# Fewer changes of the array's form, the rows s = 0 with weights fixed, and a reordered head and tail in a Fourier-mixing and maxout kernel

## The chip, the cores and the metric

The kernel runs on one core of a Trainium2 chip. Its engines are TensorE (PE in the profile, with its weight loads as PEld), VectorE (DVE), ScalarE (ACT), GpSimd (POOL) and SyncE (SP, which here only issues DMAs). The metric is the device time of one execution in microseconds (us); of several runs the median is taken. The profile is that of one execution.

## The reference

```python
def _attn_ref(x):                      # x: (8, 3072, 256)
    X = np.fft.fft(x, axis=1)
    X = np.fft.fft(X, axis=2)
    return X.real.astype(np.float32)

def _moe_ref(x, w1, w2, w3, w_out):    # x: (24576, 256), w: (256, 768), w_out: (768, 256)
    h = np.maximum(np.maximum(x @ w1, x @ w2), x @ w3)
    return (h @ w_out).astype(np.float32)
```

The real part of a two-dimensional Fourier transform over 3072 rows and 256 columns is taken for each of 8 batches, and its 8 x 3072 rows go through a small network: three products with 768 columns each, the largest of the three at each place, and a product with `w_out`.

## The kernel before

The kernel folds the transform over the 256 columns into the weights: `w1`, `w2`, `w3` are multiplied once, in the head, by cosine tables (`g_all`, `gd_all`, `gw`). What is left for each batch is the transform over the rows, in stages, and the network.

**Stage one** (`Mix.s`, line 390) multiplies x by a table `tab` of 64 columns. Since 64 columns fill half of the 128 x 128 array, each of the pieces s0 to s5 is a pair of matmuls that run side by side in the two halves of the array (`tile_position=(0, 0)` and `(0, 64)`), 512 columns each. The piece s6 holds one single row of x that is left over and is one matmul of 128 columns in one half. A copy takes each piece out of PSUM. The stores `y0`, `y1` and the loads `z0`, `z1` (issued on SP) then turn the result by way of DRAM, and **stage two** (`Mix.k`) multiplies it by sine and cosine tables into `tE` and `tO`. The first row of each batch, s = 0, is kept apart in `t_mid` and is written alone (`out[S*b]`).

**The units.** A batch has 18 units: three blocks (`blk`) of 512 columns times six blocks of 128 hidden columns (`jc`). The loop at line 898 writes out the order of a unit by hand: `begin` (the products for the rows counted upwards, `hp`), `finish` of the unit before (those counted downwards, `hm`), `third` for a unit two further on, one scatter of finished rows at units 0, 4, 8 and 14 (`PACE`), ten steps of the product with `w_out` (`l2_some`), and then what the plan has for this unit (`at`, `piece`). All engines keep this order: each takes its instructions in the order of the program.

A unit is either *plain*, with six matmuls of 512 columns on TensorE (`unit_plus` four, `unit_minus` two), two relus on ACT and two maxima on DVE, or *split*, with five matmuls: `third` gives two of them to its own PSUM tiles `e3` and `d3`, DVE adds a rank-one term (`even3`), ACT scales (`odd3`), and POOL makes the sum and the difference of the two (`plus3`, `minus3`, line 867), which DVE then needs at lines 879 and 892. Odd units are split from unit 7 of batch 0 on; even ones where `EXTRA` says so: 12 and 14 in batch 0, then 0, 4, 8, 12 and 14, and 0, 4, 8 and 12 in the last batch.

The tiles `e3`, `d3`, those of stage one, of stage two and of the even part `pl` share three PSUM buffers (`ps_f`). The plain units and the split even units share one buffer for the third product (`ps_w3`), all odd ones and the plain ones two others (`ps_l1`).

**The plan of stage one.** For batch 0 the pieces of batch 1 lie in four units (`ahead0`). For the batches 1 to 6 the pieces of the next batch lie in three units (`ahead`): s0 and s1 in unit 1; s2, s3 and s6 in unit 2; s4 and s5 in unit 3.

**The rows s = 0** (`l2_mid`, line 620) are computed for all batches together in the last batch: hidden values in unit 1, the product with `gw` and `w_out` in unit 3. There the 8 values of a batch row are the weights (128 x 8) and `gw` or `wout_bf` stream, 256 columns in each of eight matmuls; one store of 8 rows follows.

**The head** (lines 150 to 330 and 674 to 739). POOL makes index ramps (`iota`, `ramp`) and issues all the loads; x of batch 0 comes in four parts, each of which DVE mirrors (`mirror`, line 124) before stage one of it can run. POOL also clears a part of the buffer `tb`, between two groups of weight loads. DVE makes the signs `sgn` and `dif` between two mirrors. Then DVE transposes `tb` (line 427), and the first units follow. POOL computes the last third of the angles (`angle`) after all that. `column` (line 348) turns one row of `g_all` into a column by six matmuls with a single row of the array.

**The tail.** In the last batch POOL makes two reversed copies of `tE` and `tO` at the start of unit 12 (line 911); `l2_last` uses them to write the last block in four parts, so that stores run while the rest is computed. The rows counted downwards leave by indirect DMAs from POOL (`scatter`, line 654); the last batch has one each at units 0, 4, 8, 14 and 16, and the rest at the end.

Of the kernel before, what the change touches and what calls it, by code (L numbers as in the profile page):

```python
# [30 lines left out]
PACE = (0, 4, 8, 14)  # L31
EXTRA = (12, 14), (0, 4, 8, 12, 14), (0, 4, 8, 12)

# [12 lines left out]
def kernel(  # L46
# [43 lines left out]
    x0u = consts.tile([128, 160], BF16, tag="x0u")  # L90
    tab = consts.tile([128, 64], BF16, tag="tab")
    tabx = consts.tile([128, 2 * RI], BF16, tag="tabx")
# [95 lines left out]
    for k in range(3):  # L188
        load_w(k, 0, 128)
    nc.gpsimd.memset(tbw[:, :, 24:32], 0)  # L190
    for k in range(3):
        load_w(k, 128, 384)
    ramp(2)

    zero = gen.tile([128, 512], BF16, tag="zero")
    nc.vector.memset(zero, 0.0)
    nc.vector.memset(x0u, 0.0)
    one = consts.tile([1, 1], BF16, tag="one")
    nc.vector.memset(one, 1.0)
    half_pi = gen.tile([128, 1], FP32, tag="half_pi")  # L200
    nc.vector.memset(half_pi, 0.5 * math.pi)
    nc.scalar.activation(out=half_pi, in_=half_pi, func=AX.Sin)
    nc.vector.memset(half_pi, 0.5 * math.pi)
    ang_o = gen.tile([128, NA], FP32, tag="ang_o")
    nc.vector.memset(ang_o, 0.0)
# [142 lines left out]
    def column():  # L348

        psc = ps_f.tile([128, 512], FP32, name="psc", tag="ps")  # L350
        for jc in range(NJC):
            nc.tensor.matmul(psc[:, jc:jc + 1], g_all[0:1, jc, 3, :], one, start=True, stop=True)
        nc.scalar.copy(out=wcol, in_=psc[:, 0:NJC])
# [27 lines left out]
    class Mix:  # L381
# [8 lines left out]
        def s(self, k, pool=ps_f, evict=nc.scalar.copy):  # L390
            ps1 = pool.tile([128, 512], FP32, name="ps1", tag="ps")
            if k < 6:
                for hh in range(2):
                    nc.tensor.matmul(ps1[hh * 64:hh * 64 + 64], tab,  # L394
                                     self.x[:, 8 * k + hh:8 * k + 8:2, 0:128],
                                     start=True, stop=True, tile_position=(0, 64 * hh))
                if self.b:
                    evict(out=tbv[:, 4 * k:4 * k + 4, :],
                          in_=ps1.rearrange("p (s f) -> p s f", s=4))
                else:  # L400
                    evict(out=tbt[:, :, 4 * k:4 * k + 4, :],
                          in_=ps1.rearrange("p (s f l) -> p f s l", s=4, l=2))
            else:
                nc.tensor.matmul(ps1[0:64, 0:128], tab, self.x[:, 48, 0:128],
                                 start=True, stop=True, tile_position=(0, 0))
                if self.b:
                    evict(out=tbv[0:64, 24, :], in_=ps1[0:64, 0:128])
                else:
                    evict(out=tbt[0:64, :, 24, :],
                          in_=ps1[0:64, 0:128].rearrange("p (f l) -> p f l", l=2))  # L410
# [209 lines left out]
    def l2_mid():  # L620
# [16 lines left out]
        po = ps_f.tile([128, 512], FP32, name="pom", tag="ps")  # L637
        for k in range(2):
            nc.tensor.matmul(po[0:B, 0:256], t_mid[:, k, :], gw[:, k * 256:(k + 1) * 256],
                             start=(k == 0), stop=(k == 1))  # L640
        for _ in l2_hidden(po[0:B, 0:256], lambda jc: hmid[:, jc, :]):
            pass
        ot = even_pool.tile([128, 512], FP32, name="even", tag="even")
        nc.vector.tensor_copy(out=ot[0:B, 0:256], in_=po[0:B, 0:256])
        store(nc.sync, out[0: S * (B - 1) + 1: S, :], ot[0:B, 0:256])

# [37 lines left out]
    warm_up(1)  # L684
    scal(sgn, pidx, 0.0, ALU.is_equal)
    scal(sgn, sgn, 2.0, ALU.mult, -1.0, ALU.add)
    scal(dif, sgn, 1.0, ALU.subtract)
    mirror(0, *FIRST[3])
# [48 lines left out]
    differ(0, 2, 128, 384)  # L737
    m.f()
    angle()

    def rows():

        pool = nc.gpsimd
        rows_f = gen.tile([128, 4], FP32, tag="rows_f")
        adj = gen.tile([128, 4], FP32, tag="adj")
        far = gen.tile([128, 1], FP32, tag="far")
        for (c, n, base, cm) in ((0, 2, 766, -8), (2, 1, 3069, -32), (3, 1, 3056, -16)):
            iota(rows_f[:, c:c + n], [[-1, n]], base=base, cm=cm)
        for (c, base, cm) in ((0, 766, 0), (1, 511, 0), (2, 1013, 0), (3, 1025, -16)):
            iota(adj[:, c:c + 1], [[0, 1]], base=base, cm=cm)  # L750
        scal(far, pidx, 96.0, ALU.is_ge, eng=pool)
        scal(adj, adj, far, ALU.mult, eng=pool)
        pool.tensor_tensor(out=rows_f, in0=rows_f, in1=adj, op=ALU.add)
        nc.gpsimd.tensor_copy(rows_m, rows_f)

# [65 lines left out]
    for b in range(2, B):  # L821
# [3 lines left out]
        for ch in range(8):  # L825
# [5 lines left out]
              15: ("v1", "kE1"), 16: ("kO2",), 17: ("v2", "kE2", "end")}  # L831
    ahead = {1: ("s0", "s1"), 2: ("s2", "y0", "s3", "s6"), 3: ("s4", "s5", "y1", "u"),
             5: ("z0", "z1"), 11: ("x",), 12: ("kO0",), 13: ("v0", "kE0", "kO1"),
# [64 lines left out]
    for g in range(B * UNITS):  # L898
# [20 lines left out]
        for lead in (1, 2):  # L919
            if is_split(g + lead) and (lead == 1) == (g + lead == 7):  # L920
                third(g + lead)
        if u in PACE or (b == B - 1 and u == 16):
            scatter(1)
        l2_some(10)
# [44 lines left out]
```

## Time and profile before

| | us |
|---|---|
| median of 3 runs (lowest, highest) | 386.15 (385.78, 387.81) |
| the profiled execution | 386.05 |
| its span, from the first to the last instruction | 384.2 |
| TensorE busy | 372.2 |
| DVE busy | 336.9 |
| POOL busy | 334.3 |
| ACT busy | 242.5 |

All times in the profile count from the start of the span. A line of a timeline gives start, length, engine, line of the code, operation, output and input, and in brackets the idle time of the engine just before, with the instruction that ended it. Matmuls overlap: the length of one is its flight, and the distance of two starts is what one costs in a stream. A line of the windows gives a stretch, its length, the busy time of PE, PEld, DVE, ACT and POOL with the count of instructions, the granted TensorE clock, the busy share of the DMA engines and the GB/s that they moved. A line of the waits gives engine and line, what it waited for, the total, the number and the longest; "issue" stands for idle time that nothing in the profile explains.

### The profile page before, as it was taken

The numbers are of one execution on the slowest core, as the hardware profiler recorded it, in microseconds if no ns is written. First come the engines' busy times: TensorE is split into PE (matmuls) and PEld (weight loads), VectorE is DVE, ScalarE is ACT, GpSimd is POOL, SyncE is SP. The second block draws the span as 40 slices with busy tenths as digits, with TensorE's granted clock in tenths as the row PEclk, the third lists the DMA queues.
The fourth block names the chain that finished last, engine by engine and source line by source line (L and its number), as shares of the span: only waits on it lengthen the run. The fifth ranks groups of instructions, "written<-read, shape, count | busy, mean of one in ns | idle before, by whom it ended". The sixth has DMA issues, their size and how long they took to land.

```text
span 384.2 us, 8003 instructions
## 1 busy us (share of the span) xinstructions
PE 372.2 (97%) x2785; PEld 234.6 (61%) x2785; DVE 336.9 (88%) x568; ACT 242.5 (63%) x454; POOL 334.3 (87%) x356
## 2 busy tenths in 40 slices
PE   6699999999999999999999999999999999999995
PEld 2354566566765667556665666666665667666674
DVE  7889798799897998989987998989987998989982
ACT  6877788567857686567766777567856535434430
POOL 9976599969999899989999899989988899888971
PEclk9999999999999999999999999999999999999999
DMA  8999836695279735595269825695213633212226
GB/s 117 169 185 164 160 117 97 202 156 178 73 155 199 203 113 115 161 218 176 69 123 199 214 105 124 179 182 183 93 56 124 178 129 97 73 67 97 97 80 209
DMA packets 51299, 54.13 MB, mean 141 GB/s; under 512 B 25813, under 2 KB 44268, under 8 KB 50563
## 3 DMA queue, kind: packets, MB, share of 16 engines
q0 software_dynamic: 19392, 26.45, 34.2%
q1 hardware_dynamic: 31334, 26.57, 25.7%
q10 hardware_dynamic: 532, 0.59, 0.5%
q8 instruction: 22, 0.36, 0.4%
q14 instruction: 19, 0.16, 0.1%
HBM read 36.95 MB, written 30.81 MB: 176 GB/s over the span
## 4 chain that ended last, share of the span: by engine, by line
PE 90%; DVE 3%; DMA 2%; ACT 2%; issue 1%; POOL 1%; DVEq 0%; POOLq 0%
PE po L550 32%; PE pse L494 10%; PE pse L487 8%; PE pse L877 6%; PE pse L878 6%; PE e L858 6%; PE d L860 6%; PE po L573 5%; PE ps L460 3%; PE ps L394 3%; PE pl L566 3%; DMA xt<-in_x_dram 2%; DVE yb L427 1%; ACT stmp L500 1%; PE psg L311 1%
## 5 line engine op out<-in xcount | busy, mean ns | idle before, releaser
L867 POOL TENSOR_TENSOR plus<-even,odd 128x512 bf16<-128x512 f32 x105 | 133.4, 1271 | 31.4 <-DVE even L863 25.8
L867 POOL TENSOR_TENSOR minus<-even,odd 128x512 bf16<-128x512 f32 x105 | 133.5, 1272 | 0.0
L862 ACT ACTIVATE odd<-d 128x512 f32<-128x512 f32 x105 | 62.7, 597 | 60.4 <-PE d L860 47.6
L879 DVE SCALAR_TENSOR_TENSOR hp<-pse,plus 128x512 bf16<-128x512 f32 x105 | 72.2, 687 | 25.0 <-PE pse L878 22.8
L550 PE MATMUL po<-wout_bf,hp 128*128 128x256 bf16 x576 | 86.1, 273 | 0.0
L550 PE MATMUL po<-wout_bf,hm 128*128 128x256 bf16 x576 | 78.6, 273 | 0.0
L863 DVE SCALAR_TENSOR_TENSOR even<-vb,wcol,e 128x512 f32<-128x512 bf16 x105 | 77.4, 737 | 0.0
L550 PEld LDWEIGHTS <-hp 128*128 128x128 bf16 x576 | 56.3, 98 | 26.2
L892 DVE SCALAR_TENSOR_TENSOR hm<-pse,minus 128x512 bf16<-128x512 f32 x105 | 71.4, 680 | 0.4
L550 PEld LDWEIGHTS <-hm 128*128 128x128 bf16 x576 | 56.3, 98 | 16.4
L494 PE MATMUL pse<-tO,gd_all 128*128 128x512 bf16 x183 | 63.1, 380 | 0.0
L500 ACT ACTIVATE stmp<-pse 128x512 bf16<-128x512 f32 x78 | 46.3, 599 | 21.2 <-PE pse L487 10.3
L578 DVE TENSOR_TENSOR kq<-po,even 128x512 f32<-128x512 f32 x60 | 41.0, 683 | 0.0
L129 ACT COPY xt<-xt 64x762 bf16<-64x762 bf16 (+1 forms) x48 | 39.8, 838 | 1.0
L877 PE MATMUL pse<-tE,g_all 128*128 128x512 bf16 x105 | 39.9, 380 | 0.1
L858 PE MATMUL e<-tE,g_all 128*128 128x512 bf16 x105 | 39.8, 379 | 0.0
L860 PE MATMUL d<-tO,gd_all 128*128 128x512 bf16 x105 | 39.8, 379 | 0.0
L878 PE MATMUL pse<-tO,g_all 128*128 128x512 bf16 x105 | 39.8, 379 | 0.0
L573 PE MATMUL po<-gw,tO 128*128 128x512 bf16 x92 | 34.9, 379 | 0.0
L570 ACT COPY even<-pl 128x512 f32<-128x512 f32 x46 | 26.8, 582 | 9.5 <-DVE kq L578 7.8
L501 DVE TENSOR_TENSOR hp<-pse,stmp 128x512 bf16<-128x512 f32 x39 | 26.8, 686 | 5.7 <-PE e L858 2.1
L494 PEld LDWEIGHTS <-gd_all 128*128 128x128 bf16 x183 | 17.9, 98 | 20.3 <-issue 2.5
(182 smaller groups left out, 500.2 us busy)
## 6 DMA issues: line engine op xcount, KB each, us to landing
db<-tb SPq DMA_DIRECT2D x21, 192.0 KB
xt<-in_x_dram POOLq DMA_DIRECT2D x5, 784.0 KB, 7.7
xt<-in_x_dram POOLq DMA_DIRECT2D x5, 752.0 KB, 8.6
out_dram<-obuf SPq DMA_DIRECT2D x8, 384.0 KB
out_dram<-kq SPq DMA_DIRECT2D x8, 384.0 KB
vb<-vd SPq DMA_DIRECT2D x23, 128.0 KB
out_dram<-kq SPq DMA_DIRECT2D x7, 288.0 KB
out_dram<-kq SPq DMA_DIRECT2D x15, 128.0 KB
```

The source lines that it names most:

```text
L494: nc.tensor.matmul(pse, gd_all[:, jc, i, :], to, start=False, stop=True, skip_group_check=True)
L550: nc.tensor.matmul(po, hcols(jc), wout_bf[:, jc * 256:(jc + 1) * 256], start=False, stop=(jc == NJC - 1), skip_group_check=True)
L573: nc.tensor.matmul(po, to[:, cp], gw[:, 256:768], start=True, stop=True)
L858: nc.tensor.matmul(e3, g_all[:, jc, 2, :], te, start=True, stop=True)
L860: nc.tensor.matmul(d3, gd_all[:, jc, 1, :], to, start=True, stop=True)
L862: nc.scalar.activation(out=odd3, in_=d3, func=AX.Copy, scale=-0.5)
L863: nc.vector.scalar_tensor_tensor(out=even3, in0=vb, scalar=wcol[:, jc:jc + 1], in1=e3, op0=ALU.mult, op1=ALU.add)
L867: nc.gpsimd.tensor_tensor(out=dst, in0=even3, in1=odd3, op=op)
L877: nc.tensor.matmul(pse2, g_all[:, jc, 0, :], te, start=True, stop=False)
L878: nc.tensor.matmul(pse2, g_all[:, jc, 1, :], to, start=False, stop=True)
L879: nc.vector.scalar_tensor_tensor(out=dst, in0=pse2, scalar=0.0, in1=sums[g][0], op0=ALU.max, op1=ALU.max)
L892: nc.vector.scalar_tensor_tensor(out=dst, in0=pses[0], scalar=0.0, in1=sums.pop(g)[1], op0=ALU.max, op1=ALU.max)
```

## The change

- `EXTRA`: unit 14 of the last batch is split as well.
- `tab` has 128 columns; `rows` (POOL, unit 5 of batch 0) copies the first 64 into the second 64. From batch 1 on the single row s6 is a matmul of the whole array, with 128 weight columns.
- `ahead`: s0, s1, s2 and y0 in unit 1; s3, s4, s5 in unit 2; s6, y1 and u in unit 3.
- `one` is a column of 128 with a one on top, and `column` uses the whole array.
- `l2_mid`: the blocks of `gw` and `wout_bf` (128 x 128) are the weights and the 8 values stream; sixteen matmuls give the result with the output columns on the partitions. DVE copies 128 x 16 values, and two stores write them with single elements of 4 bytes.
- Head: POOL's clearing of `tb` becomes a copy of zeros on ACT; `ramp(2)` moves from behind the weight loads to just before `angle`; the three instructions for `sgn` and `dif` move from DVE to POOL.
- `scatter`: the last batch has one each at units 0, 4 and 8 and two at unit 16; none at 14.

```diff
-EXTRA = (12, 14), (0, 4, 8, 12, 14), (0, 4, 8, 12)
+EXTRA = (12, 14), (0, 4, 8, 12, 14), (0, 4, 8, 12, 14)
...
-    tab = consts.tile([128, 64], BF16, tag="tab")
+    tab = consts.tile([128, 128], BF16, tag="tab")
...
-    nc.gpsimd.memset(tbw[:, :, 24:32], 0)
     for k in range(3):
         load_w(k, 128, 384)
-    ramp(2)
...
-    one = consts.tile([1, 1], BF16, tag="one")
-    nc.vector.memset(one, 1.0)
+    one = consts.tile([128, 1], BF16, tag="one")
+    nc.vector.memset(one, 0.0)
+    nc.vector.memset(one[0:1], 1.0)
...
+    nc.scalar.copy(out=tbt[:, :, 24:32, :], in_=zero[:, 0:16].rearrange("p (s l) -> p s l", l=2)
+                   .unsqueeze(1).to_broadcast([128, 64, 8, 2]))
...
-            nc.tensor.matmul(psc[:, jc:jc + 1], g_all[0:1, jc, 3, :], one, start=True, stop=True)
+            nc.tensor.matmul(psc[:, jc:jc + 1], g_all[:, jc, 3, :], one, start=True, stop=True)
...
-                    nc.tensor.matmul(ps1[hh * 64:hh * 64 + 64], tab,
+                    nc.tensor.matmul(ps1[hh * 64:hh * 64 + 64], tab[:, 0:64],
...
-                nc.tensor.matmul(ps1[0:64, 0:128], tab, self.x[:, 48, 0:128],
-                                 start=True, stop=True, tile_position=(0, 0))
+                n = 128 if self.b else 64
+                nc.tensor.matmul(ps1[0:n, 0:128], tab[:, 0:n], self.x[:, 48, 0:128],
+                                 start=True, stop=True)
...
-        for k in range(2):
-            nc.tensor.matmul(po[0:B, 0:256], t_mid[:, k, :], gw[:, k * 256:(k + 1) * 256],
-                             start=(k == 0), stop=(k == 1))
-        for _ in l2_hidden(po[0:B, 0:256], lambda jc: hmid[:, jc, :]):
-            pass
+        for h in range(2):
+            steps = [(gw[:, 256 * k + 128 * h:256 * k + 128 * h + 128], t_mid[:, k, :])
+                     for k in range(2)]
+            steps += [(wout_bf[:, 256 * jc + 128 * h:256 * jc + 128 * h + 128], hmid[:, jc, :])
+                      for jc in range(NJC)]
+            for k, (w, v) in enumerate(steps):
+                nc.tensor.matmul(po[:, h * B:h * B + B], w, v,
+                                 start=(k == 0), stop=(k == len(steps) - 1))
...
-        nc.vector.tensor_copy(out=ot[0:B, 0:256], in_=po[0:B, 0:256])
-        store(nc.sync, out[0: S * (B - 1) + 1: S, :], ot[0:B, 0:256])
+        nc.vector.tensor_copy(out=ot[:, 0:2 * B], in_=po[:, 0:2 * B])
+        for h in range(2):
+            store(nc.sync, out[0:S * (B - 1) + 1:S, 128 * h:128 * h + 128].rearrange("b p -> p b"),
+                  ot[:, h * B:h * B + B])
...
-    scal(sgn, pidx, 0.0, ALU.is_equal)
-    scal(sgn, sgn, 2.0, ALU.mult, -1.0, ALU.add)
-    scal(dif, sgn, 1.0, ALU.subtract)
+    scal(sgn, pidx, 0.0, ALU.is_equal, eng=nc.gpsimd)
+    scal(sgn, sgn, 2.0, ALU.mult, -1.0, ALU.add, eng=nc.gpsimd)
+    scal(dif, sgn, 1.0, ALU.subtract, eng=nc.gpsimd)
...
     m.f()
+    ramp(2)
     angle()
...
-        nc.gpsimd.tensor_copy(rows_m, rows_f)
+        pool.tensor_copy(rows_m, rows_f)
+        pool.tensor_copy(tab[:, 64:128], tab[:, 0:64])
...
-    ahead = {1: ("s0", "s1"), 2: ("s2", "y0", "s3", "s6"), 3: ("s4", "s5", "y1", "u"),
+    ahead = {1: ("s0", "s1", "s2", "y0"), 2: ("s3", "s4", "s5"), 3: ("s6", "y1", "u"),
...
-        if u in PACE or (b == B - 1 and u == 16):
-            scatter(1)
+        if b < B - 1:
+            scatter(u in PACE)
+        else:
+            scatter({0: 1, 4: 1, 8: 1, 16: 2}.get(u, 0))
```

## The prediction

> **What bounds the kernel now.** I read the page first (busy times, then the chain that ended last), then the table of windows for one batch in the middle.
>
> ```profile
> PE 372.2 (97%) x2785; PEld 234.6 (61%) x2785; DVE 336.9 (88%) x568; ACT 242.5 (63%) x454; POOL 334.3 (87%) x356
> ...
> PE 90%; DVE 3%; DMA 2%; ACT 2%; issue 1%; POOL 1%; DVEq 0%; POOLq 0%
> ```
> ```profile
> 92.52:136.37 43.85, 43.85 (x330) 27.78 (x329) 39.38 (x63) 30.93 (x57) 40.58 (x39) 1.00 0.66 158
> ```
> TensorE is busy for all 43.85 us of batch 2, at full clock (1.00), while DVE works 39.38 and POOL 40.58 us of them. So in the middle a shorter TensorE programme is a shorter kernel, as long as POOL and DVE, each with some 3 us to spare per batch, do not come to stand in front. Head and tail have other limits and are read on their own.
>
> What a matmul costs in a stream, from the chain in order of time:
>
> ```profile
> 48.53 0.86 PE pse L487 x4
> ...
> 52.21 1.09 PE po L550 x10
> ```
> So 512 columns take 0.215 us, 256 columns 0.109 us.
>
> **Stage one in two groups instead of three (batches 1 to 6).** The TensorE timeline at a group of today:
>
> ```profile
> 115.85 0.38 PE L550 MATMUL po<-wout_bf,hp 128*128 128x256 bf16 x2
> 116.16 0.62 PE L394 MATMUL ps<-xt,tab 128*64 128x512 bf16 x4
> 116.71 0.39 PE L494 MATMUL pse<-tO,gd_all 128*128 128x512 bf16 x1
> ```
> The two 256-column matmuls free the array at 115.85 + 2 x 0.109 = 116.07, yet the group starts at 116.16: 0.09 us to enter. Its two pieces run as pairs of half-arrays (128*64), 2 x 0.215 = 0.43 us, to 116.59; the next whole-array matmul starts at 116.71: 0.12 us to leave. A group costs 0.21 us beside its work. The waits say that this happens at every group:
>
> ```profile
> PEld L394 <- issue: 4.7, 22, 0.3
> ```
> 22 entries are four in batch 0 and three in each of batches 1 to 6. The change makes two of three: s0 to s2 in unit 1, s3 to s5 in unit 2, and s6, now with 128 weight columns, as an ordinary matmul in unit 3 with the same 128 columns streamed. Gain 6 x 0.21 = 1.26 us. The lower bound on that gain is zero, if the buffers take it back: three pieces in a row use all three PSUM buffers that `third` and the even part also use.
>
> ```profile
> 116.61 1.07 ACT L398 CAST tb<-ps 128x512 bf16<-128x512 f32 x2 [0.75 <-PE po L550]
> 117.57 0.61 ACT L500 ACTIVATE stmp<-pse 128x512 bf16<-128x512 f32 x1
> 118.82 0.74 DVE L863 SCALAR_TENSOR_TENSOR even<-vb,wcol,e 128x512 f32<-128x512 bf16 x1
> ```
> ACT's third copy pushes its relu from 117.57 to about 118.1, and the DVE behind it: `even` for unit 4 ends near 120.1 instead of 119.56. The last piece of the new second group (s5) would start at about 120.07 and needs that buffer. That is a stall of under 0.1 us; I count none, and keep up to 0.2 us a batch for the range. The DMA y0 is issued one unit earlier on SP, with no store in front of it that changes; nobody waits for its end before the z loads.
>
> In batch 0 the piece s6 stands behind s5 as before: one entry, one exit, nothing gained. It now waits for `rows` on POOL, which copies the second half of `tab` in unit 5, a unit before; POOL has no split unit there yet.
>
> **The row s = 0.** Today eight matmuls with eight weight columns (128*8, another form of the array) stream 256 columns each; afterwards sixteen with 128 weight columns stream 8. The nearest row for the new form is in the same function: 24 matmuls of 128x8.
>
> ```profile
> 335.21 0.17 PE L628 MATMUL psm<-t_mid,g_all 128*128 128x8 bf16 x1
> ...
> 335.79 0.17 PE L630 MATMUL psm<-t_mid,g_all 128*128 128x8 bf16 x1
> 335.82 0.38 PE L494 MATMUL pse<-tO,gd_all 128*128 128x512 bf16 x1
> ```
> ```profile
> 340.14 0.82 PE L550 MATMUL po<-wout_bf,hp 128*128 128x256 bf16 x6
> 340.89 0.38 PE L639 MATMUL pom<-gw,t_mid 128*8 128x256 bf16 x2
> ...
> 341.86 0.39 PE L877 MATMUL pse<-tE,g_all 128*128 128x512 bf16 x1
> ```
> 24 in 0.61 us are 0.025 us each, so 16 take 0.40. Today the stretch runs from 340.14 + 6 x 0.109 = 340.79 to 341.86, 1.07 us with its switches. Gain 0.67 us. The row's matmuls add in twos into the same columns, the new ones in eights; the other end is that each waits out the flight of the one before, 0.17 us, which makes 2.7 us and a loss of 1.6. The twos don't wait, so I take the row. The result lies transposed, so two stores put 4-byte elements, 2 x 1024 of them, on SP's queue.
>
> ```profile
> q1 hardware_dynamic: 31334, 26.57, 25.7%
> ```
> ```profile
> 344.49 3.37 SPq L509 DMA_DIRECT2D out_dram<-kq  x3
> ```
> 25.7% of 16 x 384.2 us over 31334 packets are 50 ns a packet: 2048 of them take 6.4 us if 16 engines share them. Behind them on SP stand those three stores; their buffer is written again only in the last block, so I count nothing. [...]
>
> `column` becomes six whole-array matmuls; its 0.1 us lies in batch 0 ahead of work that DVE holds back. Nothing.
>
> **The head.** Three small DVE instructions go to POOL. They stand between two mirror copies on the chain:
>
> ```profile
> 12.55 0.15 DVE L220 TENSOR_SCALAR sgn<-pidx 128x1 f32<-128x1 f32 x1
> ...
> 13.12 0.90 DVE L129 COPY xt<-xt 64x1143 bf16<-64x1143 bf16 x1
> ```
> ```profile
> 7.25 0.60 POOL L122 DMA_DIRECT2D xt<-in_x_dram  x1
> ```
> ```profile
> xt<-in_x_dram POOLq DMA_DIRECT2D x1, 128.0 KB, 5.8
> ```
> Up to 13.12 - 12.55 = 0.57 us could go. But the last part of x, issued at 7.25, lands 5.8 us later, at 13.05, and the mirror that reads it starts at 13.12: the three instructions fill a wait for a DMA. I take 0 (ends: 0 and -0.57). The other moves have cover:
>
> ```profile
> 5.03 0.81 ACT L245 ACTIVATE kq<-kq,phi,s_of 128x512 f32<-128x512 f32 x1 [2.80 <-POOL kq L145]
> ```
> ```profile
> 12.84 1.14 POOL L145 IOTA kq<- 128x288 f32 x4
> 26.90 1.56 POOL L129 COPY xt<-xt 64x1651 bf16<-64x1651 bf16 x1 [1.99 <-DMA xt<-in_x_dram]
> ```
> The zeros, now an ACT copy, fall into ACT's wait of 2.80 us; the ramp (1.14 us) goes behind the weight and x(1) loads, which POOL then issues some 0.5 to 1 us earlier, and before `angle`; its end shifts into POOL's 1.99 us wait. The loads are limited by the DMA engines, so their earlier issue brings nothing.
>
> **Unit 14 of the last batch split.** TensorE saves one of six 512-column matmuls, 0.22 us. But POOL gets two more sums, just behind the two flip copies:
>
> ```profile
> 361.47 1.27 POOL L867 TENSOR_TENSOR minus<-even,odd 128x512 bf16<-128x512 f32 x1
> 362.69 0.61 POOL L911 COPY tEr<-tE 128x512 bf16<-128x512 bf16 x1
> 363.24 0.61 POOL L911 COPY tOr<-tO 128x512 bf16<-128x512 bf16 x1
> 364.19 1.27 POOL L867 TENSOR_TENSOR plus<-even,odd 128x512 bf16<-128x512 f32 x1 [0.34 <-DVE even L863]
> 365.42 1.27 POOL L867 TENSOR_TENSOR minus<-even,odd 128x512 bf16<-128x512 f32 x1
> 366.83 0.99 POOL L654 DMA_INDIRECT out_dram<-kq,rows_m  x1 [0.15 <-issue]
> ```
> ```profile
> 366.44 0.69 DVE L879 SCALAR_TENSOR_TENSOR hp<-pse,plus 128x512 bf16<-128x512 f32 x1 [0.60 <-PE pse L878]
> ...
> 369.08 0.68 DVE L892 SCALAR_TENSOR_TENSOR hm<-pse,minus 128x512 bf16<-128x512 f32 x1
> 369.67 0.68 DVE L501 TENSOR_TENSOR hp<-pse,stmp 128x512 bf16<-128x512 f32 x1
> ```
> ```profile
> 370.72 0.59 PE L494 MATMUL pse<-tO,gd_all 128*128 128x512 bf16 x2
> ```
> On today's clock: flips end 363.85; the sums of unit 14 follow at a pitch of 365.42 - 364.19 = 1.23, so the `plus` of unit 15 starts at 366.31 and ends at 367.58 (today 365.46). DVE's hp of unit 15, today at 366.44, waits for it: 1.15 us late. Behind it in DVE's order come hm 14, even 17, a block sum and hm 15, at some 0.6 us each, then hp 16, which ends near 371.35 instead of 370.35. TensorE's second L494 of unit 16 (today 370.93) needs that read done: about 371.4. So the saved 0.22 becomes +0.47 us at the end. Ends: -0.22 if POOL keeps up after all, +1.15 if the whole lag passes on. Taking the scatter out of unit 14 (366.83) is already used here; it gives POOL 1.1 us before the sums of unit 17.
>
> The sums of unit 17 wait for even 17, near 369.5, and end near 372; that scatter and the one of unit 16 follow at about 372 and 373, the last at 374. The DMA engines there:
>
> ```profile
> 374.00:376.00 2.00, 2.00 (x21) 1.80 (x19) 0.69 (x1) 0.00 (x0) 0.46 (x2) 1.00 0.97 287
> 376.00:378.00 2.00, 2.00 (x21) 1.80 (x19) 0.79 (x2) 0.00 (x0) 0.57 (x1) 1.00 0.88 316
> ```
> They are 97% and 88% busy. Half a megabyte (128 rows of 4 KB) that comes into this stretch is up to 1.7 us at 316 GB/s; the stretch behind has room and the last stores shift too. I take +0.2 (ends 0 and +1.7).
>
> **Sum.** -1.26 - 0.67 + 0.47 + 0.2 = -1.26 us against the profiled execution of 386.05 (span 384.2 and 1.85 around it): 384.8. The median of the runs, 386.15, is 0.1 above it: 384.9 us, 0.3% less. About 0.5% (1.9 us) is what a measurement tells from no change, so this is "same".
>
> **Rivals.** (1) The tail costs nothing: unit 14 gains its 0.22 and the scatters hide; 386.15 - 1.26 - 0.67 - 0.22 = 384.0, faster. For it: DVE has 0.60 us idle before hp 15. Against it: POOL's order above. 0.23. (2) The head was held by DVE after all, -0.57: 384.3, just short of 0.5%, and with (1) 383.4. Against it stands the landing at 13.05. 0.12. (3) Stage one doesn't do what it says: buffers or ACT take back what the switch gave; 386.15 - 0.67 + 0.67 = 386.15, same. Stalls would show at L394 with ACT or DVE as releaser. 0.1. (4) Slower: the 4-byte stores, at 342 in the last batch, end after everything else. Sixteen engines leave 128 packets each; with 40 us to the end a packet must take over 310 ns, or fewer than three engines share them at 50 ns. On one engine 2048 x 0.05 = 102 us would end at 445: some 449 us. 0.07. The forecast has 0.48.
>
> **How the numbers follow.** Faster: (1) and two thirds of (2), 0.31. Slower: (4), 0.07. Same: the rest, 0.62. The range, 383.4 to 386.4, reaches from both gains of (1) and (2) to (3) with 0.2 us more, and leaves out (4) and the corners.
>
> **What would show it.** After: 16 entries of L394 put down to issue; the TensorE time of a middle batch 0.21 us shorter; sixteen pom matmuls in 0.4 us with no gap about them; the mirror at 13.1 waiting for a DMA; in the last units hp of unit 15 put down to POOL plus, over 1 us later beside TensorE than today. The prediction is wrong if that wait is missing, if L394 waits for ACT or DVE in unit 2, or if the last batch's stores land late.

## The result, and the profile after

The changed kernel takes 402.12 us (median; 400.98 to 403.05) where the kernel before takes 386.2 us in runs beside it: a ratio of 1.041 (95% interval 1.038 to 1.043), 16 us slower. The forecast was 384.9.

The page of the changed kernel, its busy times, the granted clock in 40 slices and the chain that ended last:

```profile
PE 370.6 (93%) x2744; PEld 236.7 (59%) x2792; DVE 334.4 (84%) x567; ACT 242.2 (61%) x454; POOL 336.3 (84%) x361
...
PEclk9999999999999999999999999999999999966998
...
PE 73%; DMA 10%; POOL 6%; DVE 4%; ACT 3%; issue 2%; SPq 0%; POOLq 0%; ACTq 0%; DVEq 0%
```

TensorE works 1.6 us less than before, in a span that is 15.7 us longer. The clock falls in two slices near the end, and DMA stands in the chain with 10%. The windows of the same trace show where (start and end, length, then PE, PEld, DVE, ACT, POOL, the clock, the DMA share and GB/s): one batch in the middle, and two stretches of the last batch.

```profile
93.23:136.93 43.70, 43.38 (x325) 28.05 (x329) 39.22 (x63) 30.82 (x57) 40.44 (x39) 1.00 0.68 163
...
349.00:361.00 12.00, 0.00 (x0) 0.00 (x0) 0.06 (x1) 0.26 (x1) 1.82 (x2) 0.66 0.85 52
361.00:367.00 6.00, 5.63 (x24) 3.24 (x24) 3.33 (x5) 1.42 (x3) 3.50 (x4) 0.55 0.13 51
```

The batch in the middle takes 43.70 us instead of 43.85. From 349 to 361 us no compute engine does anything to speak of while the DMA engines are 85% busy and move 52 GB/s, and then TensorE works for 6 us at a clock of 0.55. The chain in order of time (start, length, what) and the ACT and PE timelines name the cause:

```profile
342.55 18.09 DMA out_dram<-even
360.64 0.02 issue
360.66 0.04 ACTq L572
360.70 0.04 issue
360.74 0.59 ACT even L572
```
```profile
360.74 0.58 ACT L572 COPY even<-pl 128x512 f32<-128x512 f32 x1 [13.31 <-DMA out_dram<-even]
```
```profile
361.37 0.58 PE L869 MATMUL d<-tO,gd_all 128*128 128x512 bf16 x1 [12.47 <-ACT even L572]
```

The two stores of single elements take 18.09 us to land. Their source `ot` is not a buffer of its own: it is a tile named `even`, with two buffers, and the other user of these buffers is ACT's copy `even` (line 572), once per three units. That copy waits 13.31 us for the stores to be done with the buffer, and TensorE 12.47 us for the copy.

The profiled executions are 15.76 us apart (401.81 and 386.05). Of these, 12.47 are this wait, 2.7 the low clock after it (6 us at 0.55 do the work of 3.3) and 1.3 the tail (below); the row itself gives back 0.67, and the kernel was 0.05 ahead at 329 us. Together that is 15.75.

### The profile page after: what moved, and what is told of

Read it like the earlier page. It is cut to its first block, busy times and chain, and to the rows that moved or that the text cites. A ratio compares the mean times of both kernels' runs of the same rounds, so it can differ in the third digit from the quotient of the medians.

```text
span 399.9 us, 7978 instructions
## 1 busy us (share of the span) xinstructions
PE 370.6 (93%) x2744; PEld 236.7 (59%) x2792; DVE 334.4 (84%) x567; ACT 242.2 (61%) x454; POOL 336.3 (84%) x361
## 3 DMA queue, kind: packets, MB, share of 16 engines
q1 hardware_dynamic: 33398, 26.57, 28.3%
## 4 chain that ended last, share of the span: by engine, by line
PE 73%; DMA 10%; POOL 6%; DVE 4%; ACT 3%; issue 2%; SPq 0%; POOLq 0%; ACTq 0%; DVEq 0%
PE po L552 27%; PE pse L496 9%; PE pse L489 6%; PE pse L886 5%; DMA xt<-in_x_dram 5%; PE d L869 5%; PE e L867 5%; DMA out_dram<-even 5%; PE pse L887 4%; PE po L575 3%; PE ps L462 3%; POOL plus L876 2%; PE ps L395 2%; PE pl L568 2%; POOL minus L876 2%
## 5 line engine op out<-in xcount | busy, mean ns | idle before, releaser
L871 ACT ACTIVATE odd<-d 128x512 f32<-128x512 f32 x106 | 63.5, 599 | 68.2 <-PE d L869 56.9
L552 PE MATMUL po<-wout_bf,hm 128*128 128x256 bf16 x576 | 79.4, 275 | 0.0
L872 DVE SCALAR_TENSOR_TENSOR even<-vb,wcol,e 128x512 f32<-128x512 bf16 x106 | 78.4, 739 | 0.0
L901 DVE SCALAR_TENSOR_TENSOR hm<-pse,minus 128x512 bf16<-128x512 f32 x106 | 72.3, 682 | 2.1 <-PE pse L496 1.4
L502 ACT ACTIVATE stmp<-pse 128x512 bf16<-128x512 f32 x76 | 45.4, 603 | 18.9 <-PE pse L489 9.8
L503 DVE TENSOR_TENSOR hm<-pse,stmp 128x512 bf16<-128x512 f32 x38 | 26.2, 688 | 17.5 <-ACT stmp L502 16.8
L887 PE MATMUL pse<-tO,g_all 128*128 128x512 bf16 x85 | 32.4, 382 | 0.2 <-issue 0.2
L575 PE MATMUL po<-gw,tO 128*128 128x512 bf16 x80 | 30.6, 383 | 0.0
```

What stands on the lines that cost most here:

```text
L503: nc.vector.tensor_tensor(out=dst, in0=src3, in1=stmp[:, 0:n], op=ALU.max)
L552: nc.tensor.matmul(po, hcols(jc), wout_bf[:, jc * 256:(jc + 1) * 256], start=False, stop=(jc == NJC - 1), skip_group_check=True)
L871: nc.scalar.activation(out=odd3, in_=d3, func=AX.Copy, scale=-0.5)
L872: nc.vector.scalar_tensor_tensor(out=even3, in0=vb, scalar=wcol[:, jc:jc + 1], in1=e3, op0=ALU.mult, op1=ALU.add)
L887: nc.tensor.matmul(pse2, g_all[:, jc, 1, :], to, start=False, stop=True)
L901: nc.vector.scalar_tensor_tensor(out=dst, in0=pses[0], scalar=0.0, in1=sums.pop(g)[1], op0=ALU.max, op1=ALU.max)
```

## Experiments

### Which part of the change

*old_mid* is the kernel after with the row s = 0 as before; *mid_only* is the kernel before with the new row alone.

```diff
-        for h in range(2):
-            steps = [(gw[:, 256 * k + 128 * h:256 * k + 128 * h + 128], t_mid[:, k, :])
...
-            store(nc.sync, out[0:S * (B - 1) + 1:S, 128 * h:128 * h + 128].rearrange("b p -> p b"),
-                  ot[:, h * B:h * B + B])
+        for k in range(2):
+            nc.tensor.matmul(po[0:B, 0:256], t_mid[:, k, :], gw[:, k * 256:(k + 1) * 256],
+                             start=(k == 0), stop=(k == 1))
...
+        store(nc.sync, out[0: S * (B - 1) + 1: S, :], ot[0:B, 0:256])
```

> The changed kernel with the rows s = 0 computed and stored as before (8 rows on the partitions, one store of 1 KB rows), in a buffer of the even part. Theory A: the store lands in a few us, nothing waits: 386.9 + 0.65 for the longer matmuls = 387.5 us. Theory B: the same. If something else in the change makes the loss, it stays near 400 us.

> The kernel before with nothing changed but the rows s = 0 (weights fixed, two 4-byte stores, buffer of the even part). Theory A: the whole loss is here: 386.2 - 0.65 + 15.2 = 400.8 us, with ACT's even copy waiting for the store and the clock at one half behind it. If the loss needs the split of unit 14 or the regrouped stage one, under 395 us.

Measured: old_mid 387.32 us, ratio 1.0035 (1.0015 to 1.0054); mid_only 400.61 us, 1.0365 (1.0341 to 1.0389). The row s = 0 is the loss, in the kernel before as in the kernel after. What is left of the change without it costs 1.2 us (387.32 beside 386.1), where the forecast had a gain of 0.6.

### The buffer, or the stores themselves

*own_buffer* (after) and *mid_own* (before with the new row) give the result a tile of its own, so that nothing waits for the stores to read it.

```diff
-        ot = even_pool.tile([128, 512], FP32, name="even", tag="even")
+        ot = consts.tile([128, 2 * B], FP32, tag="ot")
```

> The changed kernel, but the result of the rows s = 0 lies in a tile of its own and no longer in one of the two buffers of the even part. The two 4-byte stores stay. Theory A (held buffer): ACT's copy of the even part no longer waits 13.3 us for the store, TensorE loses neither the 12.5 us nor the half-speed stretch behind it (some 2.7 us): 402.1 - 15.2 = 386.9 us, the clock back at 0.999, while the two stores still take about 18 us to land. Theory B (the DMA engines are the trouble: 2048 packets hold up every other transfer): the wait only moves to another transfer, the time stays above 395 us. Theory C (the clock falls because of the sixteen small matmuls): the half-speed stretch stays, about 390 us.

> The kernel before with the rows s = 0 with weights fixed, and their result in a tile of its own. Theory A: the saving of TensorE stays without its price: 386.2 - 0.65 = 385.55 us. Theory B: above 395 us, as in the kernel with everything.

Measured: own_buffer 396.47 us, ratio 1.0269 (1.0226 to 1.0311); mid_own 395.27 us, 1.022 (1.0186 to 1.0253). The wait for the buffer is gone, but two thirds of the loss stay: Theory A falls as the whole explanation. Theory B's number fits, but the wait did not move to another transfer, as the waits below show. Theory C falls: the clock drops here too (0.50 from 360 to 365 us), but kept_clean (below) has the same sixteen matmuls, and its granted clock is 0.998 over the whole span, where own_buffer has 0.990. The waits of own_buffer (engine, line, what it waited for, total, number, longest):

```profile
ACT odd L871 <- remote: 10.8, 1, 10.8
...
DVE hm L901 <- remote: 7.2, 1, 7.2
```

"remote" means that no signal in the trace ended the wait. DVE's `hm` needs a product that TensorE began 8 us before:

```profile
350.01 0.38 PE L496 MATMUL pse<-tO,gd_all 128*128 128x512 bf16 x1
```
```profile
358.42 0.69 DVE L901 SCALAR_TENSOR_TENSOR hm<-pse,minus 128x512 bf16<-128x512 f32 x1 [7.20 <-remote]
```

In the trace's record of signals the last one of TensorE before the gap is at 349.32, the next at 358.40, and then six come between 359.92 and 360.15, for matmuls that the trace has from 350 to 353.5. This record has holes: POOL ends three sums between 350.2 and 352.7, and none of their signals is in it. That signals of TensorE came late, and are not only missing, rests on the engines: DVE starts `hm` at 358.42 and ACT `odd` at 360.11, each right behind such a signal. So ACT and DVE stand still for signals that are some 8 us late. Meanwhile the DMA engines are stuck, though not on the single elements. The queue in own_buffer from 341 to 343 us, and then from 346 to 353 us, when only ordinary stores were left to move (packets, MB, share of 16 engines):

```profile
q1 hardware_dynamic: 998, 0.00, 22.6%
```
```profile
q1 hardware_dynamic: 30, 0.09, 91.1%
```

998 single elements take 22.6% of 16 engines for 2 us, 7 ns each. Then 30 packets of 3 KB fill 91.1% of 16 engines for 7 us, 3.4 us each. Before, in a stretch of 4 us with the same stores, such packets took 0.17 us each:

```profile
q1 hardware_dynamic: 124, 0.34, 33.0%
```

### Instruction fetches?

My next theory (D) was that the late element is an engine's next block of instructions, fetched through the same DMA engines (the page's instruction queues, q8 and q14: 22 and 19 packets before). *burst_between* and *burst_on_fetch* put a pair of such stores into the kernel before, away from its row s = 0: where no fetch falls (unit 7 of batch 5, shown), and where three do (the same in batch 4).

```diff
+        if (b, u) == (5, 7):
+            nc.vector.memset(extra, 0.0)
+            for h in range(2):
+                store(nc.sync, out[0:S * (B - 1) + 1:S, 128 * h:128 * h + 128]
+                      .rearrange("b p -> p b"), extra[:, h * B:h * B + B])
```

> The kernel before, with one more pair of stores of 2 x 1024 single 4-byte elements (zeros, to the rows s = 0, which the last batch writes anyway), issued in unit 7 of batch 5, at about 259 us. In the trace of before the DMA queues that carry instructions have no packet from 258 to 277 us. Theory D (while such stores are on their way, instruction fetches are held up with all other traffic, and the engine that needs the next block stands still): no fetch falls into this stretch, so no idle time that nothing of the kernel ended; 386 to 387.5 us. Theory E (such stores stall ACT and DVE whatever is fetched): 8 to 10 us more, some 395 us. Theory F (the stall belonged to the last batch alone): 386.2 us.

> The same pair of stores in the same unit of batch 4, at about 215.5 us. In the trace of before instruction packets come at 225.3, 225.9 and 228.9 us, inside the 18 us that such stores take. Theory D: one or more engines stand still from about 225 to the end of the stores, near 233, with no releaser in the kernel; 390 to 395 us. Theory E: some 395 us, as the other one. Theory F: 386.2 us.

Measured: 391.03 us, ratio 1.0125 (1.0085 to 1.0165), and 395.88 us, 1.0253 (1.0225 to 1.0281). Neither trace has a wait on "remote", so D is not confirmed, and the stall that E expects is not there either: in burst_on_fetch two instruction packets that before has at 224 to 226 and 228 to 230 us come at 232 to 234 and 236 to 238, 8 us late, and no engine stops for them. (The stores left at 220.4 and 264.3, 5 us later than meant.) The stall of own_buffer itself speaks against D too: there no instruction packet moves from 341 to 361 us, and DVE (358.42) and ACT (360.11) had gone on before the next one came. In the two burst runs the loss comes 21 to 22 us behind the stores, in the next batch, from a third victim. SP's timeline and the wait in burst_on_fetch:

```profile
220.44 1.89 SPq L509 DMA_DIRECT2D out_dram<-extra  x2
229.87 3.63 SPq L509 DMA_DIRECT2D out_dram<-obuf  x2
233.59 0.44 SPq L465 DMA_DIRECT2D vd<-tO  x1
241.42 0.35 SPq L469 DMA_DIRECT2D vb<-vd  x1
```
```profile
DVE even L864 <- DMA vb<-vd: 6.7, 1, 6.7
```

The next batch needs a small row `vb` on all partitions, which three pairs of small DMAs on SP make one after the other, each waiting for the one before. The first `vb` starts at 241.42; in the kernel before it starts at 233.82. In burst_between the same wait is 5.1 us. So these bursts cost where the first short chain of small DMAs has no slack, some 20 us behind them.

### Number and time

In this order: *own_half* has one of the two stores of own_buffer; *own_few* an eighth of the elements, in two of the eight rows; *own_late* copies the tile once more in unit 7 and stores it from there. The first two leave the other elements of these rows unwritten.

```diff
-        for h in range(2):
+        for h in range(1):
             store(nc.sync, out[0:S * (B - 1) + 1:S, 128 * h:128 * h + 128].rearrange("b p -> p b"),
```
```diff
+        store(nc.sync, out[0:S + 1:S, 0:128].rearrange("b p -> p b"), ot[:, 0:2])
```
```diff
+        yield
+        ot2 = consts.tile([128, 2 * B], FP32, tag="ot2")
+        nc.vector.tensor_copy(out=ot2, in_=ot)
...
+                  ot2[:, h * B:h * B + B])
...
+        if b == B - 1 and u in (1, 3, 7):
```

> The kernel after with the result of the row s = 0 in a tile of its own and only the first of its two stores: the columns 128 to 255 of these eight rows are not written. Theory G (the stall with no releaser lasts until the memory has taken the single writes, 16 us for 2048 or 7.8 ns each): 1024 writes are done at 350.4, before anything stands still; 386.7 us. Theory H (something of the program at 350 us is the cause, and any such store brings it): some 395 us. By half the loss: 391 us.

> The kernel after with the result in a tile of its own and a store of 2 x 128 single elements instead of 2 x 8 x 128: six of the eight rows s = 0 and the second half of the other two are not written. If the loss goes with the number: an eighth of 10 us, 387.5 to 388 us. If a few hundred single writes hold up the memory as long as 2048 do: 395 us or more.

> The kernel after with the result of the row in a tile of its own, copied once more by DVE in unit 7 of the last batch and stored from there, at about 349.5 instead of 341.4 us. Theory T (signals are held up from some 7 us after the first single write on): ACT and DVE stand still from about 357 to 366 us instead of 350 to 360; some 396 us. Theory P (a place of the program at 350 us meets the store): the store is then only beginning, no stall without a releaser; 387 to 390 us.

Measured: own_half 397.9 us, ratio 1.0301 (1.0276 to 1.0325); own_few 386.34 us, 1.0007 (0.9995 to 1.0019); own_late 393.97 us, 1.0208 (1.0185 to 1.0231). So 1024 writes cost as much as 2048, and 256 cost nothing that the runs can tell: the price is not one per packet, and Theory G falls. (own_few also writes two rows instead of eight; whether the number of elements or that of rows spares it was not tried.) In own_half the signals of TensorE stop at 349.30 and come again at 361.72, later than with twice the writes (ACT waits 12.6 us on "remote", DVE 10.0). In own_late the stall moves with the store (issued 10 us later than in own_buffer): the signals stop at 359.77 and come again at 366.94, and the waits are

```profile
ACT odd L874 <- remote: 6.0, 1, 6.0
...
DVE hp L891 <- remote: 5.3, 1, 5.3
```

so Theory T holds and P falls, and with P the H of own_half, whose number alone fitted. Shown is, for the last batch: some 8 us after such a store of 1024 or 2048 elements was issued, TensorE's signals stop coming (7.9 us in own_buffer and own_half, 8.4 in own_late) until the DMA engines move again (own_buffer: 22 GB/s from 350 to 355 us, 349 from 360 to 362). Not shown is by which way the one holds up the other, nor why the bursts in the middle of the kernel had no such effect. Every run here was recorded; whether the recording has a share in what is left of the loss in own_buffer, no run shows.

### The parts that were forecast to gain

*stage_only*, *head_only* and *tail_only* are the kernel before with one part each, in this order:

```diff
+                n = 128 if self.b else 64
+                nc.tensor.matmul(ps1[0:n, 0:128], tab[:, 0:n], self.x[:, 48, 0:128],
...
+            nc.tensor.matmul(psc[:, jc:jc + 1], g_all[:, jc, 3, :], one, start=True, stop=True)
...
+    ahead = {1: ("s0", "s1", "s2", "y0"), 2: ("s3", "s4", "s5"), 3: ("s6", "y1", "u"),
```
```diff
-    nc.gpsimd.memset(tbw[:, :, 24:32], 0)
...
+    nc.scalar.copy(out=tbt[:, :, 24:32, :], in_=zero[:, 0:16].rearrange("p (s l) -> p s l", l=2)
...
+    scal(sgn, pidx, 0.0, ALU.is_equal, eng=nc.gpsimd)
...
+    ramp(2)
     angle()
```
```diff
+EXTRA = (12, 14), (0, 4, 8, 12, 14), (0, 4, 8, 12, 14)
...
+            scatter({0: 1, 4: 1, 8: 1, 16: 2}.get(u, 0))
```

*kept_oldcol* and *kept_s6* each take a piece of stage one back, in the kernel *kept_clean* of the next part:

```diff
+            nc.tensor.matmul(psc[:, jc:jc + 1], g_all[0:1, jc, 3, :], one, start=True, stop=True)
```
```diff
-                n = 128 if self.b else 64
+                n = 128 if self.b > 1 else 64
```

> The kernel before with stage one in two groups, the row s6 and the column on the whole array, alone. The prediction: 386.15 - 1.26 = 384.9 us. From the milestones of the traces (0.15 us less in each of batches 1 to 6, 0.43 us more in batch 0): 385.7 us.

> The kernel before with the moves of the head alone (zeros on ACT, ramp before the angles, three small instructions on POOL). The prediction: no change (386.1). The trace of after had its first milestone 0.25 us later and the second 0.68 us later, of which stage one and the column could be a part: by that 386.4 to 386.8 us.

> The kernel before with unit 14 of the last batch split and the scatters moved, alone. The prediction: 0.47 for the late sum of POOL and 0.2 for the scatters, 386.8 us. If the saved matmul is all that counts: 385.9 us. From the run with the old row (387.3), which was 0.05 us ahead of before at 329 us and ended 1.2 us behind: 387.4 us.

> kept_clean (385.2 us) with the column as before, six matmuls with one row of the array. If the column makes the wait of 0.37 us in batch 0: 384.8 us and no wait of TensorE at 57.8 us. If not: 385.2 us, the wait stays.

> kept_clean (385.2 us) with the row s6 of batch 1 in half the array, as before; from batch 2 on as in kept_clean. If that row's wait for the copied table makes the wait of 0.37 us in batch 0: 384.8 us and no wait at 57.8 us. If not: 385.2 us.

Measured: stage_only 385.95 us beside 386.19, ratio 0.9994 (0.9983 to 1.0004); head_only 386.03 beside 386.42, 0.9987 (0.9978 to 0.9997); tail_only 387.43 beside 386.42, 1.0024 (1.0012 to 1.0035); kept_oldcol 384.85, 0.997 (0.9958 to 0.9982); kept_s6 385.04, 0.9966 (0.9954 to 0.9978). The last two lie inside each other's interval and that of kept_clean; only the traces tell them apart. kept_oldcol's number is the one expected if the column made the wait, and its trace shows that it does not: the fit is luck. TensorE's timeline in batch 0 of stage_only, of kept_oldcol and of kept_s6:

```profile
57.97 0.43 PE L462 MATMUL ps<-to_tab,yb 128*128 128x32 bf16 x8 [0.37 <-DVE even L866]
```
```profile
57.73 0.43 PE L463 MATMUL ps<-to_tab,yb 128*128 128x32 bf16 x8 [0.37 <-DVE even L873]
```
```profile
57.72 0.43 PE L464 MATMUL ps<-to_tab,yb 128*128 128x32 bf16 x8
```

The wait for a PSUM buffer goes only with the row s6 of batch 1. Between the same matmul of two batches (the one with a single column, line 475 before) batch 0 takes 35.59 us in stage_only, 35.07 in kept_s6 and 35.16 before. So the new form of that one row costs 0.4 to 0.5 us there; the column costs nothing.

### A version that keeps what gains

*row_turned* is the kernel after with the result turned by DVE before the store; *kept_parts* has, of the change, stage one, the column and the turned row, with head and tail as before; *kept_clean* clears the tile early; *kept_head* adds the head's moves.

```diff
-        nc.vector.tensor_copy(out=ot[:, 0:2 * B], in_=po[:, 0:2 * B])
-        for h in range(2):
-            store(nc.sync, out[0:S * (B - 1) + 1:S, 128 * h:128 * h + 128].rearrange("b p -> p b"),
-                  ot[:, h * B:h * B + B])
+        nc.vector.tensor_copy(out=ot[:, :, 0:B], in_=po[:, 0:2 * B].rearrange("p (h b) -> p h b", h=2))
+        nc.vector.transpose(out=otr.rearrange("p h b -> p (h b)"), in_=ot.rearrange("p h b -> p (h b)"))
+        for a in range(4):
+            store(nc.sync, out[0:S * (B - 1) + 1:S, :]
+                  .rearrange("b (h a j) -> a b h j", h=2, a=4)[a], otr[32 * a:32 * a + B])
```

The 24 columns of `ot` that stay empty are cleared; row_turned and kept_parts do it in `l2_mid` (first line), kept_clean and kept_head in `rows` (second line):

```diff
-        nc.gpsimd.memset(ot, 0.0)
+        pool.memset(ot, 0.0)
```

> The kernel after, but the result of the row s = 0 is turned by DVE (32 x 32 blocks) before it is stored, so that 64 pieces of 128 bytes leave instead of 2048 of 4 bytes. If all of the loss is the 4-byte stores: the run with the old row (387.3) less the 0.67 us that the new matmuls save, 386.7 us; if something else of the new row costs, 388 us or more.

> The kernel before with stage one in two groups, the whole-array column and row s6, and the row s = 0 with weights fixed and its result turned before the store; head and tail as before. By the traces so far: 386.15 - 6 x 0.15 (groups) - 0.67 (row) = 384.6 us. If the groups give nothing, 385.5 us.

> As kept_parts, but the tile for the turned result is cleared in batch 0. In kept_parts DVE waited 2.16 us for that clearing, which stood on POOL behind two sums, and it gave back at 342 what was won before: the row ended 0.95 us earlier than before, the kernel 0.85 us later. Without that wait: 386.1 - 0.46 (stage one, as measured at 329 us) - 0.67 (row) + 0.1 (the turn on DVE) = 385.1 us. If the wait was not the cause, 386.8 us again.

> kept_clean (stage one, column and the row turned before its store; 385.2 us) with the head's moves as well. From head_only (0.4 us below before): 384.8 us. If the 0.4 lay in the spread: 385.2 us.

Measured: row_turned 388.98 us, ratio 1.0075 (1.006 to 1.0089); kept_parts 386.8, 1.0019 (1.0002 to 1.0036); kept_clean 385.21 beside 386.42, 0.9974 (0.9961 to 0.9988); kept_head 384.85 beside 386.37, 0.9958 (0.9944 to 0.9971). The first two missed their forecasts by 2.2 us. In both, my own clearing of the tile on POOL put this wait in front of DVE:

```profile
DVE ot L651 <- POOL ot L642: 2.2, 1, 2.2
```

kept_clean, without it, has 1.6 of the 2.2 back. The turned row then costs DVE 0.24 us more and SP four issues, and 64 pieces of 128 bytes hold nothing up:

```profile
341.50 0.24 DVE L651 STREAM_TRANSPOSE otr<-ot 128x64 f32<-128x64 f32 x1
```
```profile
341.77 1.31 SPq L513 DMA_DIRECT2D out_dram<-otr  x4
```

kept_head beats both kernels: 1.5 us below before, 17 below after.

## Why the prediction was wrong, step by step

**The stores of the row s = 0: the step that failed.** The prediction costed the two stores at nothing, because "Behind them on SP stand those three stores; their buffer is written again only in the last block". That names the cover of the stores *behind* them, not that of their own source. `ot` has the tag `even`, and the next writer of that buffer is ACT, which is ready for it at 347.4, 5 us after the stores were issued. The question that should have been asked is who next writes the tile, and the answer was on the page of the kernel before:

```profile
L570 ACT COPY even<-pl 128x512 f32<-128x512 f32 x46 | 26.8, 582 | 9.5 <-DVE kq L578 7.8
```

The size was off too: 6.4 us against 18.09 measured; even 6.4 us, from 342.55 on, would have held ACT by some 1.5. The count of packets was near: the queue q1 has 33398 instead of 31334, 2064 more where the forecast has 2048. But no price per packet would have given the rest: the elements themselves took 7 ns each, less than the 50 of the forecast, and their landing 18.09 us. Behind them the 3 KB packets of other stores take 3.4 instead of 0.17 us (own_buffer, 346 to 353 us), the signals come late, and 1024 elements cost what 2048 do.

**The last rival.** It named these stores, at 0.07, but had them harm only by ending after everything else, "a packet must take over 310 ns". That point was never reached; the harm came from what had to wait on the way. With its mechanism wrong its time (449) was as well. The sign to look for was named, though: "if the last batch's stores land late".

**The row's matmuls.** Forecast 0.40 us for sixteen; measured from 340.75 to 341.16, with the following matmul directly behind. The size and the gain of 0.67 were right; whether accumulation waits out a flight, the other end, is settled for these sixteen: they don't. From the first matmul of `l2_mid` to the last of the program TensorE takes 44.19 us before and 43.52 in kept_clean, 0.67 less.

```profile
340.75 0.19 PE L646 MATMUL pom<-t_mid,gw 128*128 128x8 bf16 x2
...
341.16 0.38 PE L886 MATMUL pse<-tE,g_all 128*128 128x512 bf16 x1
```

**Stage one: mis-sized.** Forecast 1.26, 0.21 for each of six batches. Measured in stage_only are 0.15 us in each of the six (43.70 instead of 43.85, and so on), which is 0.9, less the 0.4 to 0.5 in batch 0. The part alone is 0.2 us faster, which its interval does not tell from no change; its trace is 0.47 ahead at 329 us. The signs forecast are there (15 entries of line 395 put down to issue, forecast 16). The groups of after:

```profile
116.56 0.38 PE L552 MATMUL po<-wout_bf,hp 128*128 128x256 bf16 x2
116.87 0.84 PE L395 MATMUL ps<-xt,tab 128*64 128x512 bf16 x6
117.65 0.39 PE L496 MATMUL pse<-tO,gd_all 128*128 128x512 bf16 x1
...
120.36 0.87 PE L395 MATMUL ps<-xt,tab 128*64 128x512 bf16 x6
121.16 0.39 PE L886 MATMUL pse<-tE,g_all 128*128 128x512 bf16 x1
```

Three pieces take 3 x 0.215 = 0.645 us, so leaving costs 117.65 - 116.87 - 0.645 = 0.135 and 121.16 - 120.36 - 0.645 = 0.155 us, not 0.12. With 0.09 to enter, the two groups cost 0.47 us where three cost 0.63: the step that was mis-sized is the assumption that a group of three costs no more to leave than one of two. No wait for ACT or DVE stands at these lines in a middle batch: the feared stall did not come there. "In batch 0 ... nothing gained" overlooked that it could lose: a wait of 0.37 us for one of the three PSUM buffers, 17 us behind the changed row. Why the changed row moves that buffer was not tried.

**The head.** Near. In after the mirror waits for the load, as forecast, which lands at 13.7 instead of 13.05. The limit of the loads that the forecast names shows before as a share of the DMA engines of 1.02 to 1.48 from 7 to 15 us. head_only is 0.4 us faster (0.1 to 0.9), where the forecast had nothing, with ends of 0 and 0.57.

```profile
13.72 0.49 DVE L129 COPY xt<-xt 64x1143 bf16<-64x1143 bf16 x1 [1.18 <-DMA xt<-in_x_dram]
```

The forecast did not ask how long the mirror takes: 0.90 us before, 0.48 in head_only, whose next copy out of stage one starts at 14.53 instead of 14.91. In after, with the same moves, it starts at 14.80. Why the mirror is shorter, and what in the head gains, was not tried.

**The tail.** One term was right for its reason, the other mis-sized. Forecast 0.47 + 0.2 = 0.67; tail_only costs 0.5 to 1.4 us. The wait of DVE for POOL's sum came as described:

```profile
DVE hp L879 <- POOL plus L867: 1.2, 1, 1.2
```

and it costs TensorE what was forecast: from the first matmul of `l2_mid` to the last of the program it takes 44.67 us in tail_only and in old_mid, 44.19 before and in stage_only. That is 0.48 for the 0.47. In tail_only this hardly shows at the last six matmuls (378.89, and 378.86 before), because its head was 0.44 us early. The rest of the cost is behind TensorE. The windows of the end in tail_only, and the last stretch before:

```profile
376.00:378.00 2.00, 2.00 (x21) 1.80 (x19) 0.76 (x2) 0.00 (x0) 0.56 (x1) 1.00 1.03 406
378.00:380.00 2.00, 1.71 (x16) 1.22 (x13) 1.30 (x3) 0.00 (x0) 0.54 (x1) 1.00 1.00 281
...
382.00:384.00 2.00, 0.00 (x0) 0.00 (x0) 0.00 (x0) 0.00 (x0) 0.00 (x0) 0.98 0.42 128
```
```profile
382.00:384.00 2.00, 0.00 (x0) 0.00 (x0) 0.00 (x0) 0.00 (x0) 0.00 (x0) 0.84 0.09 28
```

The DMA engines are full to 380 us and still 42% busy from 382 to 384, where they were 9% busy before. With half a megabyte moved behind 372 us the span ends 6.13 us after the start of the last matmul instead of 4.78: 1.35 us. In the eight traces with the moved scatters it ends 5.56 to 6.32 us after it, in the twelve without 4.49 to 5.19. The bounds had it (0 to 1.7), and the value taken, 0.2, lay near the wrong end.

**The sum.** Without the stores the forecast of -0.59 (stage one and tail) stands against +1.2 measured in old_mid: up to 329 us its trace has gained 0.36 instead of 1.26, behind that it has lost 1.29 instead of 0.67, and the rest is spread between executions (its head was 0.3 us later, and heads of unchanged code differ by up to 0.6). So even without the harm of the stores it would have been "same", at the upper end of the range (386.4): own_few, which is nearly that kernel, has 386.34, and old_mid less the 0.67 of the row 386.65.

## What to carry to other kernels

Before a store with a non-contiguous last dimension is called hidden, ask three things of the profile: who next writes its source buffer, which small DMAs must land while it is on its way, and what the DMA engines' share in that stretch is; and rather turn the result on the chip, which cost 0.24 us of DVE here against 16 us. A transfer that is moved towards the end should be priced by the DMA engines' share there: half a megabyte brought into stretches that were 88 to 97% busy cost 0.8 to 1.35 us, where 0.2 was taken. A saving in one stage should be priced from the whole group, entry and exit, and the buffer rotation behind it be read in every batch whose plan differs.

## What the runs showed of the hardware

- Behind 2 x 1024 single elements of 4 bytes, which took 7 ns each in the record (own_buffer, 341 to 343 us), the 3 KB packets of other stores took 3.4 us (346 to 353 us in own_buffer; 0.17 before), and the stores of the elements landed after 18.09 us (in after). 1024 elements cost as much time (own_half 397.9 us beside 396.47 in own_buffer), 256 (in two rows) none that the runs can tell (own_few, 386.34).
- In that state signals of TensorE came some 8 us late in own_buffer (none in the record from 349.32 to 358.40), with the matmuls already run by the trace (the one of 350.01 is read by DVE at 358.42); among the waits only "remote" shows it (ACT 10.8 us, DVE 7.2). The cause is open.
- In burst_on_fetch two instruction packets came 8 us late (232 to 234 and 236 to 238 us instead of 224 to 226 and 228 to 230) without any engine stopping for them.
- After 12.47 us without work TensorE was granted half its clock for 5.5 us in the kernel after (361.37 to 366.87: a distance of 0.43 instead of 0.215 us between 512-column matmuls); after 7.11 us in own_buffer, for 4.7 us (360.76 to 365.41).
